# One queue's order at the end of each attention step, and who splits the last operands

## Chip, cores and metric

One core of a Trainium2 chip runs the whole program. The time is the device time of one execution in microseconds (us); the kernel before has a median of 931.12 us over three runs (930.95 to 933.09).

## What is computed

Attention with capped scores, then a feed-forward block with a gate. With q, k, v of 8 batches x 12 heads x 448 rows x 64:

```python
scores = cap * tanh((q @ k.T) / 8 / cap)
attn = softmax(scores)                     # plus 1e-9 in the denominator
x = concat_heads(attn @ v)                 # 8 x 448 x 768
x_prev = x shifted by one row in each sequence, zero first
xk = mu_k * x + (1 - mu_k) * x_prev
xr = mu_r * x + (1 - mu_r) * x_prev
k = relu(xk @ w_k)                         # 768 -> 1024
out = sigmoid(xr @ w_r) * (k * k @ w_v)    # 1024 -> 768
```

Products are made at more than single-pass accuracy: each operand is split into a high part and a remainder, and three products are summed.

## The kernel before

The first half of the program, some 560 us, is attention with the product xk @ w_k folded in. It runs in steps i = 0 to 54. A step works on several pairs of heads at once (48 pairs, six to a batch): scores, tanh, exponential and row sums of pair i, the product with v and the reciprocal sums of pair i-1, normalising and mixing of pair i-2. The key product "K" of a batch follows about seven steps behind. TensorE does scores (`s`, L211), values (`pv`, L238 and L246) and K (`kps`, L369). ScalarE does tanh (L219), exponential (L229), the old half of the mix (`pv<-x`, L290), relu (`ko`, L376) and issues the stores of k (L382). VectorE does row sums (`r<-p`, L255), the reciprocal (`sr`, L264), normalising (`x<-pv,r`, L280), the mix (`xk`, L295) and the new half of the gate operand (`xg`, L307). GpSimd splits q, k and xk (`xkh`, `xkl`) and makes the old half of `xg` (L313). The second half, from 564 us, is the two large products with w_v and w_r (`ps`, L561), with weights in seven combinations of quadrants.

Every engine takes its instructions in order, and the order within a step is written out by hand in the tables `STEP`, `STEP_0` (steps 0 to 5), `STEP_6` (6 to 13) and `STEP_2`. SyncE's queue holds nearly all transfers. Those of a step, in order:

- `gather` (L260): four transfers that bring the row sums `r` of the pair before to one place, `sq`. The reciprocal waits for them; they wait for the last row sums `red3` of the step before.
- `load_v` (L165), `weight_load` (L400, L405; steps 0 to 41).
- `rec_store` (L271), after the reciprocal; `load_qk` (L161); `rec_load` (L276, two transfers), which brings the reciprocals back spread over partitions, for normalising in the next step.
- `x_store`, at the end of the step: it stores the gate operand `xg` of pair i-2 (L324), or for the first twelve and the last two pairs x itself (L326). It waits for `gate_new`, the last VectorE instruction of the step.
- `weight_store` (L466), and in steps 43 to 46 `quad_load` (L663): two loads of quadrants of w_v per step, 384 KB each.

The next step's `gather` comes behind all of these. The program gives its transfers eight completion semaphores in turn, SyncE's and ScalarE's counted together, and a transfer is issued only when the one eight places ahead of it has landed.

Quadrants are summed on VectorE (`quad_sum`, L670, four subtractions in step 46 and four in step 48), and the sums are split by ScalarE (high, L676) and VectorE (low, L677): 14 splittings, three before step 49, four after it, four in step 50 at the places called `prep`, and the last three in a row at the end of step 50. The last four use quadrants P1 and P2, loaded by `w2_load` (L481) when step 48 opens the tail.

Of the kernel before, what the change touches and what calls it, by code (L numbers as in the profile page):

```python
# [21 lines left out]
NF = DF // 128  # L22
ND = DM // 128
NT = B * S
NPAIR = B * NP
HN = DM // 2
# [12 lines left out]
QUADS = REST[-1] + 2  # L39
# [14 lines left out]

STEP = """gather load_v weight_load weight_low S0 S1 V S2 f f f f f tanh0 exp0 red0
weight_sum tanh1 exp1 red1 norm recip rec_store K qk_high qk_low tanh2 relu mix_old k_store prep mix_new x_high x_low gate_old
K exp2 red2 weight_rest weight_sum relu k_store prep S3 K prep K tanh3 exp3 red3 gate_new relu k_store prep
weight_abs load_qk rec_load tail_open x_store weight_store quad_load"""  # L60
STEP_2 = STEP.replace("K qk_high", "K S3 qk_high").replace("prep S3 K", "prep K")
STEP_0 = """gather load_v weight_load weight_low S0 S1 V S2 f f f f f norm tanh0 exp0 red0
weight_sum tanh1 exp1 red1 recip rec_store K qk_high qk_low tanh2 relu exp2 mix_old k_store mix_new x_high x_low gate_old
K red2 weight_rest weight_sum relu k_store S3 K K tanh3 exp3 red3 gate_new relu k_store weight_abs load_qk rec_load x_store weight_store"""
STEP_6 = """gather load_v weight_load weight_low S0 S1 V S2 f f f f f norm tanh0 exp0 red0
weight_sum tanh1 exp1 K relu_early qk_rise tanh2 relu exp2 mix_old k_store mix_new red1 recip rec_store qk_low x_high x_low gate_old
K red2 weight_rest weight_sum relu k_store S3 K K tanh3 exp3 red3 gate_new relu k_store weight_abs load_qk rec_load x_store weight_store"""


def f(ap):  # L70
    return ap.bitcast(F32)


class Body:
# [437 lines left out]
    def half(self, u):  # L512
        return (NF if u < NU else ND) // 2
# [140 lines left out]
    def quad_load(self, j):  # L654
        if j == 0:
            w = lambda: self.wp.tile([P, WC, 2], U32, name="w64", bufs=3).rearrange("p n t -> p (n t)").bitcast(F32)
            half = lambda name, t, bufs: [f(self.wp.tile([P, WC], t, name=name, bufs=bufs)).rearrange("p (f n) -> p f n", f=2) for _ in range(2)]
            whole = [w().rearrange("p (f n) -> p f n", f=NF // 2) for _ in range(3)]
            self.quad = [[x[:, k:k + 2] for k in (0, 2)] for x in whole] + [half("wsq", F32, 3), half("wa", U32, 2)]
        k = j // 2  # L660
        for q in ((0, 1), (2, 3))[j % 2]:
            c, h = ND + q // 2 * (NF // 2) + 2 * k, (0, 1, 1, 0)[q]
            self.nc.sync.dma_start(self.quad[q][k], self.w_d[c:c + 2, :, h * HN:(h + 1) * HN].rearrange("c p n -> p c n"))  # L663
            self.summed = [0, 0]

    def quad_sum(self, j):
        k = j // 2
# [17 lines left out]

    def step(self, i, KS):

        nk = 0
        if self.maxima and i < NPAIR:
            self.row_maxima(i)  # L690
        pair = dict(load_qk=i + 3, qk_high=i + 2, qk_low=i + 2, qk_rise=i + 2, load_v=i, S=i, tanh=i, exp=i, red=i)
        pair.update(dict.fromkeys("V gather recip rec_store rec_load".split(), i - 1))
        pair.update(dict.fromkeys("norm mix_old mix_new x_high x_low gate_old gate_new x_store".split(), i - 2))
        for op in (STEP_0 if i < 6 else STEP_6 if i < REST[0] else STEP_2 if i % NP == 2 else STEP).split():
            j = pair.get(op)
            op, g = (op[:-1], (int(op[-1]),)) if op[-1].isdigit() else (op, ())
            if op in pair:
                j = pair[op] if j is None else j
                if 0 <= j < NPAIR:
                    getattr(self, dict(S="scores", V="values").get(op, op))(j, *g)  # L700
            elif op == "K":
                n = ((i - LAG) * 4 + nk + 1) * KS
                if 0 <= n < B * NF * ND * 3:
                    self.kpart(n, n + KS)
                nk += 1
            elif op == "tail_open":
                self.tail_open(i)
            elif op == "f":
                if i in (QUADS + 3, QUADS + 5):
                    self.quad_sum(i - QUADS - 3)  # L710
                elif i <= NPAIR:
                    self.fill()
            elif op == "quad_load":
                if QUADS <= i < QUADS + 4:
                    self.quad_load(i - QUADS)
            elif op == "relu_early":
                if i % NP == 2:
                    self.relu()
            elif op == "weight_load":
                if i in KEYS or i in REST:  # L720
                    self.weight_load()
            else:
                getattr(self, op)()

    def run(self):
# [7 lines left out]
        with ExitStack() as outer:  # L733
            def pool(name, bufs, stack=outer, **kw):
                return stack.enter_context(tc.tile_pool(name=name, bufs=bufs, **kw))
# [40 lines left out]
            tail = NPAIR + 1  # L776
            self.later, self.prep_now = [], False
            first = -12
            tiles = dict(right, reuse_waits="tile")

            def tail_open():
                ast.close()
                self.w2v = {"l": pool("w2vl", 1, **tiles)}
                self.w2_pool("v", "l", self.w2v)
                for q in (0, 3):
                    for k in (0, 2):
                        self.w2_load("v", q, slice(k, k + 2))
            self.open_tail = tail_open
            for i in range(NPAIR + LAG):
                if i == tail:  # L790
                    est.close()
                    self.w2v["h"] = pool("w2vh", 1, **tiles)
                    self.w2_pool("v", "h", self.w2v)
                    self.w2 = self.w2_splits()
                    for _ in range(3):
                        next(self.w2)
                self.prep_now = i == tail + 1
                self.step(i, KS)
                if i == tail + 1:
                    assert len(list(self.w2)) == 3  # L800
                    wst.close()
                    ust.close()
                    self.srcp = pool("srcp", 2, **tiles)
                    self.sp = pool("sp", 1, **tiles)
                    self.evp = pool("evp", 1, **tiles)
                    self.opp = pool("opp", AHEAD + 1, **tiles)
                if i == tail + 2:
                    sst.close()
                    self.ps_2 = pool("ps2", 6, space=PSUM, **right)
                if i == tail:  # L810
                    for _ in range(4):
                        next(self.w2)
                if i == NPAIR // 2 and not self.maxima:
                    self.small = nc.values_load(self.flag, min_val=0, max_val=1)
                if i > tail + 1:
                    for g in range(first, min(first + 4, 0)):
                        self.ahead(g)
                    first += 4
            assert first >= 0
            self.k_store()  # L820
            kst.close()
            w2r = pool("w2r", 1)
# [77 lines left out]
```

## Time and profile before

| | us |
|---|---|
| median of three runs | 931.12 |
| the profiled execution | 929.66 |
| its span on the core | 927.7 |
| TensorE busy in the span | 891.2 (96%) |
| VectorE, ScalarE, GpSimd busy | 738.4, 639.6, 386.0 |

The 1.96 us between span and execution lie outside what the profile shows. Busy times of TensorE are modelled, since matmuls overlap; idle times in front of an instruction are given with what ended them. In a timeline row stand the start in us, the duration in us, engine, line, operation, tile written and tiles read, shape, and in brackets the idle time of the engine before it and what released it. "SPq" and "ACTq" are transfers being issued by SyncE and ScalarE.

### The profile page before, as it was taken

To read this page: it belongs to the slowest core of one execution; us is meant where nothing else is said; L and a number is where in the kernel's file an instruction comes from. 1 tells how busy PE (TensorE), PEld (TensorE's weight loads), DVE (VectorE), ACT (ScalarE), POOL (GpSimd) and SP (SyncE) were. 2 spreads that over 40 slices of the span, in tenths; PEclk is the share of its full clock that TensorE was granted. 3 is DMA by queue.
4 is the path that set the end of the run, shared out by engine and by line. 5 is a ranking of instruction groups with operands and counts; after the bars stand their busy time and mean duration, and the time that the engine had idled before them with its cause. 6 is when DMAs were issued, how large, how long until landed. Compare 5 with 4: busy or idle time off the path is not lost.

```text
span 927.7 us, 15107 instructions
## 1 busy us (share of the span) xinstructions
PE 891.2 (96%) x4986; PEld 714.5 (77%) x4986; DVE 738.4 (80%) x1254; ACT 639.6 (69%) x946; POOL 386.0 (42%) x330
## 2 busy tenths in 40 slices
PE   6888999999999999999998899999999999999997
PEld 3336666666676666677665589999999999999996
DVE  7999986888888888888867776788887766777775
ACT  7898887887878888877866565565655535555553
POOL 5574564666676766666654220000000013344430
PEclk9899999999999999999999999999999999999999
DMA  4556655666666666656555464754455636666773
GB/s 148 169 173 188 211 161 172 194 200 204 187 195 217 209 195 217 196 177 208 191 167 181 132 215 141 261 171 147 152 162 165 196 104 206 214 212 217 222 216 117
DMA packets 123655, 171.94 MB, mean 185 GB/s; under 512 B 22576, under 2 KB 107696, under 8 KB 123568
## 3 DMA queue, kind: packets, MB, share of 16 engines
q1 hardware_dynamic: 114352, 156.21, 53.7%
q10 hardware_dynamic: 9216, 14.68, 4.2%
q8 instruction: 41, 0.67, 0.3%
q14 instruction: 46, 0.38, 0.1%
HBM read 111.48 MB, written 56.60 MB: 181 GB/s over the span
## 4 chain that ended last, share of the span: by engine, by line
PE 41%; POOL 17%; DVE 11%; DMA 9%; issue 9%; ACT 6%; SPq 6%; ACTq 0%; DVEq 0%; POOLq 0%
PE ps L561 38%; POOL xg L313 4%; DMA sq<-r 4%; SPq L260 4%; POOL qkl L98 4%; POOL xkl L98 3%; DVE r L255 3%; POOL wsq L446 2%; ACT p L219 2%; ACT p L229 2%; POOL qkh L88 2%; POOL xkh L88 2%; DMA w<-wk 2%; PE kps L369 2%; DVE sr L264 2%
## 5 line engine op out<-in xcount | busy, mean ns | idle before, releaser
L255 DVE TRANSPOSE_TENSOR_REDUCE r<-p 128x28 f32<-128x896 f32 (+1 forms) x240 | 215.3, 912 | 12.0 <-ACT p L229 9.0
L229 ACT ACTIVATE p<-p,cap_t 128x896 f32<-128x896 f32 x192 | 182.2, 949 | 10.8 <-DMA sq<-r 4.6
L219 ACT ACTIVATE p<-s,scl_t 128x896 f32<-128x896 f32 x192 | 172.9, 901 | 17.8 <-PE s L211 12.7
L369 PE MATMUL kps<-xkh,wkh 128*128 128x448 f32 x372 | 140.5, 378 | 2.3 <-ACT ko L376 2.3
L369 PE MATMUL kps<-xkl,wkh 128*128 128x448 f32 x372 | 136.0, 366 | 0.9 <-POOL xkl L98 0.9
L369 PE MATMUL kps<-xkh,wkl 128*128 128x448 f32 x372 | 136.0, 366 | 0.1
L561 PE MATMUL ps<-wvh,hi 128*128 128x384 f32 x392 | 131.0, 334 | 0.0
L561 PE MATMUL ps<-wvl,hi 128*128 128x384 f32 x392 | 130.9, 334 | 0.0
L238 PE MATMUL pv<-p,rv 128*64 128x448 f32 x576 | 125.3, 572 | 4.5 <-DVE xk L295 4.5
L545 ACT CAST hi<-s 128x512 fp32r<-128x512 f32 (+1 forms) x112 | 63.6, 568 | 90.9 <-PE ps L561 79.0
L525 POOL TENSOR_TENSOR s<-src 128x384 f32<-128x384 f32 x14 | 14.3, 1019 | 258.6 <-DVE lo L546 258.6
L546 DVE TENSOR_TENSOR lo<-s,hi 128x512 fp32r<-128x512 f32 (+1 forms) x112 | 70.1, 625 | 59.9 <-ACT hi L545 43.8
L98 POOL TENSOR_TENSOR qkl<-rqk,qkh 128x960 fp32r<-128x960 f32 x47 | 106.9, 2274 | 11.6 <-ACT qkh L92 8.3
L211 PE MATMUL s<-qkh 64*128 64x448 f32 (+1 forms) x336 | 84.6, 444 | 21.6 <-ACT p L219 15.9
L211 PEld LDWEIGHTS s<-qkh 64*128 64x128 f32 (+1 forms) x336 | 36.8, 187 | 81.0 <-ACT p L219 34.6
L446 POOL TENSOR_TENSOR wsq<-wa,wsq 128x384 f32<-128x384 f32 (+1 forms) x39 | 43.8, 1123 | 132.8 <-DVE wsq L439 132.8
L561 PE MATMUL ps<-wrh,hi 128*128 128x384 f32 x294 | 98.6, 335 | 0.3 <-DVE o L584 0.3
L561 PE MATMUL ps<-wrl,hi 128*128 128x384 f32 x294 | 98.5, 335 | 0.0
L238 PEld LDWEIGHTS pv<-p,rv 128*64 128x64 f32 x576 | 38.7, 142 | 68.6 <-issue 58.8
L545 ACT CAST hi<-src 128x512 fp32r<-128x512 f32 (+1 forms) x84 | 47.7, 568 | 62.8 <-PE ps L561 59.8
L369 PEld LDWEIGHTS kps<-xkh,wkh 128*128 128x128 f32 x372 | 69.8, 188 | 21.3 <-issue 13.1
L561 PE MATMUL ps<-wvh,lo 128*128 128x384 f32 x392 | 83.7, 334 | 0.0
(101 smaller groups left out, 1787.3 us busy)
## 6 DMA issues: line engine op xcount, KB each, us to landing
rqk<-qk SPq DMA_DIRECT2D x47, 480.0 KB
k_d<-ko ACTq DMA_DIRECT2D x64, 224.0 KB
src<-k_d SPq DMA_DIRECT2D x56, 256.0 KB
rv<-v SPq DMA_DIRECT2D x48, 256.0 KB
r<-rec_d SPq DMA_DIRECT2D x96, 112.0 KB
v_d<-o SPq DMA_DIRECT2D x56, 192.0 KB
src<-x_d SPq DMA_DIRECT2D x42, 256.0 KB
vl<-v_d SPq DMA_DIRECT2D x56, 192.0 KB
```

What stands on the lines that cost most here:

```text
L88: self.nc.gpsimd.tensor_scalar(out, x, 1.0, 0.0, op0=ALU.mult, op1=ALU.add)
L98: {"p": self.nc.gpsimd, "v": self.nc.vector}[e].tensor_sub(*a)
L211: nc.tensor.matmul(s[:, h, 0:S], qk[a][p, k], qk[b][p, 0:S], start=(n == 0), stop=(n == 2))
L219: self.nc.scalar.activation(p32, self.S.pop((i, g))[:, :n, 0:S], AF.Tanh, scale=self.scl_t)
L229: self.nc.scalar.activation(p32, p32, AF.Exp, scale=1.0 if self.maxima else self.cap_t)
L238: nc.tensor.matmul(pv[p, 0:S], v[:, g, h, :], ph[:, h, :], start=(g == 0), stop=False)
L255: self.nc.vector.tensor_reduce(out=out, in_=p32[p, h].rearrange("p h (b k) -> p (h b) k", k=32), axis=mybir.AxisListType.X, op=ALU.add, ap ...
L369: nc.tensor.matmul(self.kps[fc][:, 0:S], w, m[:, dc, :], start=first, stop=last)
L446: {"p": self.nc.gpsimd, "v": self.nc.vector}[e].tensor_add(sq, f(a), sq)
L545: self.nc.scalar.copy(hi, x)
L546: self.nc.vector.tensor_sub(lo, x, f(hi))
L561: self.nc.tensor.matmul(o, a[:, c, :], w[:, c, :], start=first and k == 0, stop=last and k == len(todo) - 1, skip_group_check=True)
```

## The change

- `quad_load` now issues one load each time it is called and stands twice in the step: behind `gather` and `load_v`, and again behind `rec_load`. The order of the eight loads is the same.
- `x_store` moves out of the end of the step, to behind `gather` and `load_v` of the next one (with i-3 for i-2).
- In step 49, the last with an `xk`, the high part is made by ScalarE and the low part by VectorE; before, both by GpSimd.
- The loads of P1 and P2 are issued after step 49's splittings in the program, not when the tail opens; `prep` also runs in step 51, so three splittings that ran in a row at the end of step 50 stand behind a relu of step 51.

```diff
-STEP = """gather load_v weight_load weight_low S0 S1 V S2 f f f f f tanh0 exp0 red0
+STEP = """gather load_v quad_load x_store weight_load weight_low S0 S1 V S2 f f f f f tanh0 exp0 red0
...
-weight_abs load_qk rec_load tail_open x_store weight_store quad_load"""
+weight_abs load_qk rec_load quad_load tail_open weight_store"""
...
-        k = j // 2
-        for q in ((0, 1), (2, 3))[j % 2]:
-            c, h = ND + q // 2 * (NF // 2) + 2 * k, (0, 1, 1, 0)[q]
-            self.nc.sync.dma_start(self.quad[q][k], self.w_d[c:c + 2, :, h * HN:(h + 1) * HN].rearrange("c p n -> p c n"))
-            self.summed = [0, 0]
+        k, q = divmod(j, 4)
+        c, h = ND + q // 2 * (NF // 2) + 2 * k, (0, 1, 1, 0)[q]
+        self.nc.sync.dma_start(self.quad[q][k], self.w_d[c:c + 2, :, h * HN:(h + 1) * HN].rearrange("c p n -> p c n"))
+        self.summed = [0, 0]
...
-        pair.update(dict.fromkeys("norm mix_old mix_new x_high x_low gate_old gate_new x_store".split(), i - 2))
+        pair.update(dict.fromkeys("norm mix_old mix_new x_high x_low gate_old gate_new".split(), i - 2))
+        pair["x_store"] = i - 3
...
+                if i == NPAIR + 1 and op in ("x_high", "x_low"):
+                    g = ("s",) if op == "x_high" else ("v",)
...
-                    self.quad_load(i - QUADS)
+                    self.quad_load(2 * (i - QUADS) + nq)
+                    nq += 1
...
-                for q in (0, 3):
-                    for k in (0, 2):
-                        self.w2_load("v", q, slice(k, k + 2))
...
-                self.prep_now = i == tail + 1
+                self.prep_now = i in (tail + 1, tail + 2)
                 self.step(i, KS)
                 if i == tail + 1:
-                    assert len(list(self.w2)) == 3
...
                 if i == tail:
                     for _ in range(4):
                         next(self.w2)
+                    for q in (0, 3):
+                        for k in (0, 2):
+                            self.w2_load("v", q, slice(k, k + 2))
```

SyncE's queue before, from the end of step 43 (store of the gate operand and two quadrant loads) through step 44:

```order
L276 DMA r<-rec_d_108 64x448 x2
L324 DMA x_d<-xg 128x448
L663 DMA w_5295<-w_d 128x2x384
L663 DMA w_5296<-w_d 128x2x384
L260 DMA sq_204<-r_1_200 32x112 x4
L165 DMA rv<-v 128x512
L271 DMA rec_d_109<-rs 28x32
L161 DMA rqk<-qk 128x960
L276 DMA r<-rec_d_109 64x448 x2
```

The same place in the changed program:

```order
L276 DMA r<-rec_d_108 64x448 x2
L662 DMA w_5197<-w_d 128x2x384
L260 DMA sq_204<-r_1_200 32x112 x4
L165 DMA rv<-v 128x512
L662 DMA w_5198<-w_d 128x2x384
L324 DMA x_d<-xg 128x448
L271 DMA rec_d_109<-rs 28x32
L161 DMA rqk<-qk 128x960
L276 DMA r<-rec_d_109 64x448 x2
```

Between `rec_load` and the four gathers one load stands where a store and two loads stood; the store and the other load are behind the gathers.

ScalarE before, from the mix of step 49 (`pv<-x_163`) to the second pair of relus of the last batch; `wvh` are high parts of quadrant sums, `ko` are relus:

```order
L290 ACTIVATE pv<-x_163,om_k 128x448
L676 CAST wvh_5836<-w_5295 128x768
L676 CAST wvh_5833<-w_5296 128x768 x2
L676 CAST wvh_5838<-wsq 128x768 x2
L676 CAST wvh_5834<-w_5297 128x768 x2
L676 CAST wvh_5832<-wvl_5816 128x768 x2
L676 CAST wvh_5835<-wvl_5819 128x768 x2
L376 ACTIVATE ko<-kps 128x448 x2
L382 DMA k_d<-ko 128x448 x2
L376 ACTIVATE ko<-s 128x448 x2
```

The same place in the changed program:

```order
L290 ACTIVATE pv<-x_163,om_k 128x448
L92 CAST xkh<-xk 128x448
L675 CAST wvh_5831<-w_5196 128x768
L675 CAST wvh_5828<-w_5197 128x768 x2
L675 CAST wvh_5833<-wsq 128x768 x2
L675 CAST wvh_5829<-w_5198 128x768 x2
L675 CAST wvh_5827<-wvl_5816 128x768
L376 ACTIVATE ko<-kps 128x448 x2
L382 DMA k_d<-ko 128x448 x2
L675 CAST wvh_5827<-wvl_5816 128x768
L675 CAST wvh_5830<-wvl_5819 128x768 x2
L376 ACTIVATE ko<-s 128x448 x2
```

Eight splittings and the new `xkh` stand ahead of the first relus, where eleven splittings stood; three follow the relus.

## Rows read from the trace of the kernel before

**Rows 1.** Stretches: duration, then busy us (instructions) of PE, PEld, DVE, ACT, POOL; clock; DMA.

```profile
60.00:140.00 80.00, 74.62 (x421) 48.86 (x423) 71.83 (x110) 70.03 (x87) 45.44 (x36) 1.00 0.58 185
140.00:460.00 320.00, 319.44 (x1800) 217.29 (x1797) 270.35 (x462) 259.72 (x334) 209.19 (x171) 1.00 0.62 199
460.00:560.00 100.00, 90.88 (x483) 67.73 (x483) 71.31 (x97) 62.81 (x85) 37.29 (x31) 1.00 0.54 173
```

**Rows 2.** Timeline of TensorE, 455 to 566 us: the rows with idle time before them.

```profile
475.81 2.48 PE L238 MATMUL pv<-p,rv 128*64 128x448 f32 x12 [0.26 <-DVE xk L295]
...
487.97 0.47 PE L211 MATMUL s<-qkh 64*128 64x448 f32 x2 [1.49 <-ACT p L219]
...
501.31 2.48 PE L238 MATMUL pv<-p,rv 128*64 128x448 f32 x12 [2.16 <-DVE xk L295]
...
514.51 0.47 PE L211 MATMUL s<-qkh 64*128 64x448 f32 x2 [2.55 <-ACT p L219]
...
524.92 2.48 PE L238 MATMUL pv<-p,rv 128*64 128x448 f32 x12 [0.67 <-DVE xk L295]
...
544.65 0.47 PE L369 MATMUL kps<-xkl,wkh 128*128 128x448 f32 x1 [0.93 <-POOL xkl L98]
...
549.22 0.47 PE L369 MATMUL kps<-xkh,wkh 128*128 128x448 f32 x1 [1.06 <-ACT ko L376]
```

**Rows 3.** Timeline of SyncE's queue, end of step 43 and gather of step 44.

```profile
476.53 1.13 SPq L276 DMA_DIRECT2D r<-rec_d  x2
480.49 0.33 SPq L324 DMA_DIRECT2D x_d<-xg  x1
480.90 0.93 SPq L663 DMA_DIRECT2D w<-w_d  x2
481.88 2.44 SPq L260 DMA_DIRECT2D sq<-r  x4
484.43 0.53 SPq L165 DMA_DIRECT2D rv<-v  x1
```

**Rows 4.** Timeline of VectorE, steps 43 to 45.

```profile
475.68 2.41 DVE L255 TRANSPOSE_TENSOR_REDUCE r<-p 128x28 f32<-128x896 f32 x3
479.06 1.39 DVE L307 SCALAR_TENSOR_TENSOR xg<-x,mu_r,xg 128x448 f32<-128x448 f32 x1 [0.98 <-POOL xg L313]
...
486.30 0.61 DVE L264 TENSOR_REDUCE sr<-sq 32x28 f32<-32x448 f32 x1 [3.31 <-DMA sq<-r]
...
494.69 0.58 DVE L280 TENSOR_TENSOR x<-pv,r 128x448 f32<-128x448 f32 x1
499.50 0.61 DVE L264 TENSOR_REDUCE sr<-sq 32x28 f32<-32x448 f32 x1 [4.23 <-DMA sq<-r]
```

**Rows 5.** Timeline of ScalarE, step 44, then the last splittings.

```profile
480.96 1.05 ACT L376 ACTIVATE ko<-kps 128x448 f32<-128x448 f32 x2
483.02 0.64 ACT L290 ACTIVATE pv<-x,om_k 128x448 f32<-128x448 f32 x1 [1.01 <-DVE x L280]
485.50 0.81 ACTq L382 DMA_DIRECT2D k_d<-ko  x2
486.36 1.04 ACT L229 ACTIVATE p<-p,cap_t 128x896 f32<-128x896 f32 x1 [2.70 <-DMA sq<-r]
...
545.70 3.03 ACT L676 CAST wvh<-wvl 128x768 fp32r<-128x768 f32 x4
548.63 0.96 ACT L376 ACTIVATE ko<-kps 128x448 f32<-128x448 f32 x2
```

**Rows 6.** Chain of work that ended last: start, us; a transfer runs to its landing.

```profile
78.42 4.95 DMA w<-wk
...
481.38 4.04 DMA w<-w_d
...
509.21 2.78 DMA rv<-v
```

**Rows 7.** Waits in the whole span: total us, times, longest.

```profile
ACT wsq L412 <- DMA w<-wk: 8.9, 7, 2.2
```

More of the change, by code (lines that the diff above doesn't have):

```diff
@@ L50 @@
 LATE = [*range(12), NPAIR - 2, NPAIR - 1]
-STEP = """gather load_v weight_load weight_low S0 S1 V S2 f f f f f tanh0 exp0 red0
+STEP = """gather load_v quad_load x_store weight_load weight_low S0 S1 V S2 f f f f f tanh0 exp0 red0
 weight_sum tanh1 exp1 red1 norm recip rec_store K qk_high qk_low tanh2 relu mix_old k_store prep mix_new x_high x_low gate_old
 K exp2 red2 weight_rest weight_sum relu k_store prep S3 K prep K tanh3 exp3 red3 gate_new relu k_store prep
-weight_abs load_qk rec_load tail_open x_store weight_store quad_load"""
+weight_abs load_qk rec_load quad_load tail_open weight_store"""
 STEP_2 = STEP.replace("K qk_high", "K S3 qk_high").replace("prep S3 K", "prep K")
-STEP_0 = """gather load_v weight_load weight_low S0 S1 V S2 f f f f f norm tanh0 exp0 red0
+STEP_0 = """gather load_v x_store weight_load weight_low S0 S1 V S2 f f f f f norm tanh0 exp0 red0
 weight_sum tanh1 exp1 red1 recip rec_store K qk_high qk_low tanh2 relu exp2 mix_old k_store mix_new x_high x_low gate_old
-K red2 weight_rest weight_sum relu k_store S3 K K tanh3 exp3 red3 gate_new relu k_store weight_abs load_qk rec_load x_store weight_store"""
-STEP_6 = """gather load_v weight_load weight_low S0 S1 V S2 f f f f f norm tanh0 exp0 red0
+K red2 weight_rest weight_sum relu k_store S3 K K tanh3 exp3 red3 gate_new relu k_store weight_abs load_qk rec_load weight_store"""
+STEP_6 = """gather load_v x_store weight_load weight_low S0 S1 V S2 f f f f f norm tanh0 exp0 red0
 weight_sum tanh1 exp1 K relu_early qk_rise tanh2 relu exp2 mix_old k_store mix_new red1 recip rec_store qk_low x_high x_low gate_old
-K red2 weight_rest weight_sum relu k_store S3 K K tanh3 exp3 red3 gate_new relu k_store weight_abs load_qk rec_load x_store weight_store"""
+K red2 weight_rest weight_sum relu k_store S3 K K tanh3 exp3 red3 gate_new relu k_store weight_abs load_qk rec_load weight_store"""
 def f(ap):
@@ L686, in step @@
     def step(self, i, KS):
-        nk = 0
+        nk = nq = 0
         if self.maxima and i < NPAIR:
@@ L818, in run @@
                     first += 4
-            assert first >= 0
+            assert first >= 0 and next(self.w2, None) is None
             self.k_store()
```

## The prediction, made before the changed kernel ran

> **What bounds the kernel now.** I read the busy times by stretch first. From 140 to 460 us TensorE is busy 319.44 of 320 us: nothing done to the queues there can be worth more than 0.56 us. From 60 to 140 us it lacks 5.38 us, and from 460 to 560 us, where the last pairs pass and the quadrants of w_v are loaded, 9.12 us [rows 1]. After that comes the second half, which the change does not touch. So the 9.12 us are nearly the whole prize. TensorE's timeline splits them into seven waits: values in steps 44, 46 and 48 wait for `xk` (0.26, 2.16, 0.67), scores of steps 45 and 47 wait for a tanh (1.49, 2.55), and in the last batch one K matmul waits for `xkl` (0.93) and one for a relu (1.06) [rows 2]. These seven add up to 9.12.
>
> Next, what ends late behind these waits. The reciprocal of step 44 stands 3.31 us at its gathered sums, and that of step 45 4.23 us [rows 4]; `xk` is made right behind it. The row sums that the gather of step 44 reads end at 475.68 + 2.41 = 478.09 [rows 4], but the gather is issued only at 481.88, because SyncE first waits for `gate_new` (it ends at 480.45 [rows 4]), then issues the store and two quadrant loads (0.33 and 0.93 us) and only then the four gathers (2.44 us) [rows 3]. So the gather is 3.8 us late for a store and for loads that nobody needs until step 46. A second path runs over ScalarE: its two stores of k in step 44 could go when the mix ends, 483.02 + 0.64 = 483.66, and go at 485.50 [rows 5]. By the program's turn of eight semaphores the first of them waits for the second quadrant load, which lands at 481.38 + 4.04 = 485.42 [rows 6]. The exponential behind them starts 2.70 us late [rows 5], and the tanh for which scores wait 1.49 us comes right after it.
>
> **The change part by part.** *Store and loads behind the gathers, steps 43 to 46.* The gather of step 44 can now go once `rec_load` (476.53 + 1.13 = 477.66 [rows 3]) and one load of some 0.45 us are issued: at about 478.2 for 481.88, and step 43's own gather gains as much in the same way, so I count 3.7 us or more per step. The reciprocal waits of 3.31 and 4.23 us then end earlier than their cover, which is the row sums and the normalising ahead of them on VectorE. Eight places ahead of step 44's stores of k now stand its gathers, issued by 480.7, so ScalarE's stall goes too: the exponential starts at 480.96 + 1.05 + 0.64 + 0.81 = 483.46, less 0.26 because TensorE is that much earlier, 483.2 for 486.36 [rows 2, 5].
>
> What is late next? Step 45's normalising ended 494.69 + 0.58 - 486.36 = 8.9 us behind that exponential [rows 4, 5]; now at 483.2 + 8.9 = 492.1. The reciprocal, its two small followers and the mix follow without a wait; in the trace they took from 499.50 to the values at 501.31, which `xk` released, so 1.81 us [rows 2, 4], and `xk` now ends at 493.9. TensorE took 501.31 - 475.81 = 25.5 us from the values of step 44 to those of step 46, and without its waits of 1.49 and 2.16 us 21.85. It starts 0.26 us sooner, at 475.55, so it comes there at 497.4 [rows 2]. The 2.16 us go, with 3.5 us to spare. The 2.55 us in step 47 are different: step 46 has four quadrant sums on VectorE ahead of the normalising, which stay. In the trace the scores at 514.51 start 13.2 us after `xk` of step 45 (values at 501.31 were released by it), and TensorE alone would need 10.65 (13.2 less its wait of 2.55) [rows 2]. They stop waiting once `xk` is 2.55 us ahead of the values, and I have 3.5. That is a margin of 0.9 us, so I leave 0.3 of the 2.55 and keep the whole 2.55 as the other end. Step 48's 0.67 hangs on the `xk` made behind step 47's exponential, and goes with that.
>
> *High part on ScalarE, low part on VectorE in step 49.* `xkl` costs 0.93 us today [rows 2]. TensorE now comes there 7.13 us sooner (0.26 + 1.49 + 2.16 + 2.55 + 0.67), and the `xk` that is split sooner by about as much (7.4 us in step 45: 493.9 for 501.31), so on GpSimd the lateness would stay about as it is. The edit puts a cast on ScalarE and a subtraction on VectorE instead; by the mix of the same 128x448 on ScalarE, 0.64 [rows 5], and the normalising on VectorE, 0.58 [rows 4], they take 1.2 us in a row. Both stand ahead of splittings, so neither queues. I count the 0.93 as gained; the other end is 0.
>
> *Three splittings behind a relu.* A splitting on ScalarE takes 3.03 / 4 = 0.76 us [rows 5]; three are 2.3 us. Eleven of them ran ahead of the relu at 548.63, for which TensorE waited 1.06 [rows 2]. TensorE and ScalarE both come there sooner by about the same, and ScalarE has the cast of 0.64 more: without the move 1.06 + 0.64 = 1.7 us of wait would stay, with it 1.7 - 2.3, so none. Moving the loads of P1 and P2 in the program changes their place in SyncE's queue only by one store of 0.33 us [rows 3], against a landing of 4.04 for such a load [rows 6]. I leave 0.2 for this part; the other end is the 1.06.
>
> *Store behind the gathers, steps 0 to 13.* Here ScalarE waits seven times for weights of w_k, 8.9 us in all [rows 7]. What stands ahead of that load in the queue is the same set of transfers, so its issue time stays, but the store's 224 KB now stand directly ahead of it. From a 256 KB load that lands 2.78 us after its issue and a 768 KB load that lands after 4.95 [rows 6], 224 KB are worth at most (4.95 - 2.78) x 224 / 512 = 0.95 us per load. At the least it is nothing, since the voice load ahead goes out earlier by the store's issue. I take 0.1, near the least: 7 x 0.1 = 0.7 us lost; the bound is 6.7. The Trainium skill, "DMA: Bandwidth & Descriptors", section "Issuing engines are not separate DMA queues", says that all transfers run on the same 16 engines and interleave, whoever starts them. By that rule moving a transfer only moves whose bytes go first, and the sum would take the 6.7 in full.
>
> *Steady steps 14 to 42.* TensorE has no idle time to give back. The store now needs its data behind gathers and v load, 2.44 + 0.53 us after the row sums [rows 3]; `gate_new` ends 480.45 - 478.09 = 2.4 us behind them [rows 4]. So it does not hold up what follows. I count nothing.
>
> **Sum.** 9.12 - 0.3 - 0.2 - 0.7 = 7.9 us. The profiled execution would fall from 929.66 (its span from 927.7) to 921.8. It lies 1.46 under the median of the runs, 931.12, so the median would be 923.2 us.
>
> **Rivals.** (1) *VectorE's loop in step 46.* If `xk` of step 45 is not 2.55 us ahead (a gather that lands late behind a quadrant load, as now), the wait of 2.55 stays, and being later ScalarE also keeps a relu wait of 1.06: 7.9 - 2.25 - 0.86 = 4.8 gained, 926.3 us. For it: the margin is 0.9 us. Against it: only one load, not two, stands ahead of a gather, and that is issued 3.7 us sooner. (2) *Weights in the first steps come late.* The store's bytes cost their full 6.7 in place of 0.7: 929.2 us, no change. Against it: the v load ahead is earlier by the same place in the queue. By the rule of the Trainium skill above this is the outcome; no row of the trace shows which of two transfers went first. (3) *The landing was late, not the queue.* If a gather lands when it does now whatever its issue, because a quadrant load's data is ahead of it either way, only the last two waits of rows 2 (0.93, 1.06) go: 929.8 with the 0.7 lost, no change. Against it: four issues take 2.44 us by themselves. (4) *Slower.* The store stands ahead of weight load and `rec_store` and waits for `gate_new`, which hangs on GpSimd. If that were later than the 3.0 us of gathers and v load, every microsecond would hold up 28 steady steps without slack: at 1 us, 28 lost, 951 us; it decides from (7.9 / 28 =) 0.3 us. Against it: `gate_new` ends 2.4 us behind the row sums in rows 4, with 0.98 us of waiting for GpSimd in it.
>
> **How the numbers follow.** Forecast 0.70 (921.5 to 925), rival 1 0.16, rival 2 0.05, rival 3 0.04, rival 4 0.05. About 0.3% (2.8 us, so 928.3 and 933.9) is what a measurement here can tell from no change. Faster 0.88 (forecast, rival 1, and rival 2 in part), same 0.07, slower 0.05. The range reaches down to all of 9.12 gained plus a little from the first steps, 920.8, and up past rival 1 with a start cost of 2 us, 927.8; that leaves out rivals 2 to 4.
>
> **What would show it.** TensorE idle from 460 to 560 us should be under 1 us of 100; the reciprocal's waits for gathered sums gone or under 1 us; ScalarE's stores of k in step 44 issued within 0.2 us of the mix; no relu wait after 549. Rival 1 shows as a tanh wait of over 2 us in front of step 47's scores; rival 2 as weight waits of 12 us or more on ScalarE in place of 8.9 and more idle time of TensorE from 60 to 140 us; rival 3 as gathers that still land behind a quadrant load; rival 4 as idle time of TensorE between 140 and 460 us. I would be wrong most likely in the 0.9 us margin and in the 0.1 per weight load.

## The result, and the profile of the changed kernel

The changed kernel takes 922.84 us (median of 4 runs, 921.98 to 924.59) where the kernel before takes 932.11 (4 runs, 930.95 to 933.42): ratio 0.9899, 95% interval 0.9873 to 0.9924. Two further sets of runs of it gave 924.34 (ratio 0.9908) and 924.21 (0.9901). The forecast was 923.2. The gain beside the kernel before is 9.27 us, where 7.9 was forecast.

The stretches of [rows 1], in the profile of the changed kernel (duration, busy us and instructions of PE, PEld, DVE, ACT, POOL, clock, DMA):

```profile
60.00:140.00 80.00, 72.06 (x394) 46.37 (x395) 68.42 (x103) 66.23 (x81) 43.28 (x34) 0.98 0.56 177
140.00:460.00 320.00, 319.95 (x1814) 219.00 (x1813) 275.16 (x468) 263.71 (x338) 212.02 (x175) 1.00 0.64 201
460.00:560.00 100.00, 100.00 (x537) 77.64 (x536) 73.83 (x105) 70.16 (x98) 33.44 (x28) 1.00 0.58 181
```

From 460 to 560 us TensorE is now busy without a gap: all seven waits of [rows 2] are gone. From 60 to 140 us it lacks 7.94 us where it lacked 5.38, at a granted clock of 0.98 there and 1.00 before. SyncE's queue, from the end of step 43 to the store in step 44 (answers [rows 3]):

```profile
474.67 1.12 SPq L276 DMA_DIRECT2D r<-rec_d  x2
475.88 0.54 SPq L662 DMA_DIRECT2D w<-w_d  x1
476.51 2.44 SPq L260 DMA_DIRECT2D sq<-r  x4
479.05 0.53 SPq L165 DMA_DIRECT2D rv<-v  x1
479.68 0.38 SPq L662 DMA_DIRECT2D w<-w_d  x1
480.15 0.42 SPq L324 DMA_DIRECT2D x_d<-xg  x1
```

The gathers go 0.72 us behind the end of `rec_load`, in place of 4.22 us (481.88 - 477.66), and the store finds its data ready. VectorE's reciprocals follow the normalising without a wait, answering [rows 4]:

```profile
481.58 0.59 DVE L280 TENSOR_TENSOR x<-pv,r 128x448 f32<-128x448 f32 x1
482.09 0.59 DVE L264 TENSOR_REDUCE sr<-sq 32x28 f32<-32x448 f32 x1
...
492.93 0.59 DVE L280 TENSOR_TENSOR x<-pv,r 128x448 f32<-128x448 f32 x1
493.44 0.59 DVE L264 TENSOR_REDUCE sr<-sq 32x28 f32<-32x448 f32 x1
```

On ScalarE the stores of k in step 44 go at once, and the exponential behind them follows the mix without the 2.70 us of [rows 5]:

```profile
482.66 0.33 ACTq L382 DMA_DIRECT2D k_d<-ko  x1
483.03 0.63 ACT L290 ACTIVATE pv<-x,om_k 128x448 f32<-128x448 f32 x1
483.17 0.33 ACTq L382 DMA_DIRECT2D k_d<-ko  x1
483.59 1.03 ACT L229 ACTIVATE p<-p,cap_t 128x896 f32<-128x896 f32 x1
```

### The profile page after: what moved, and what is told of

It reads as the page before. It is cut to its first block, busy times and chain, and to the rows that moved or that the text cites. A ratio compares the mean times of both kernels' runs of the same rounds, so it can differ in the third digit from the quotient of the medians.

```text
span 920.2 us, 15151 instructions
## 1 busy us (share of the span) xinstructions
PE 887.3 (96%) x4986; PEld 714.8 (78%) x4986; DVE 738.4 (80%) x1255; ACT 641.6 (70%) x947; POOL 383.4 (42%) x328
## 4 chain that ended last, share of the span: by engine, by line
PE 85%; DVE 6%; DMA 3%; ACT 3%; issue 1%; SPq 1%; DVEq 0%; ACTq 0%
PE ps L561 39%; PE kps L369 23%; PE s L211 11%; PE pv L238 10%; DVE r L255 3%; PE pv L246 2%; DMA w<-wk 2%; ACT p L219 1%; ACT p L229 1%; PE s L369 1%; DMA w<-wr 1%; DVE sr L264 0%; DVE wkl L460 0%; DVE wa L435 0%; DMA r<-rec_d 0%
## 5 line engine op out<-in xcount | busy, mean ns | idle before, releaser
L369 PE MATMUL kps<-xkh,wkh 128*128 128x448 f32 x372 | 140.3, 377 | 1.0 <-ACT ko L376 1.0
L369 PE MATMUL kps<-xkh,wkl 128*128 128x448 f32 x372 | 136.1, 366 | 0.1
L369 PE MATMUL kps<-xkl,wkh 128*128 128x448 f32 x372 | 136.0, 366 | 0.0
L238 PE MATMUL pv<-p,rv 128*64 128x448 f32 x576 | 122.9, 563 | 2.4 <-DVE xk L295 2.4
L238 PEld LDWEIGHTS pv<-p,rv 128*64 128x64 f32 x576 | 38.0, 140 | 64.5 <-issue 57.0
L369 PEld LDWEIGHTS kps<-xkh,wkh 128*128 128x128 f32 x372 | 69.8, 188 | 19.9 <-issue 12.5
```

What stands on the lines that cost most here:

```text
L238: nc.tensor.matmul(pv[p, 0:S], v[:, g, h, :], ph[:, h, :], start=(g == 0), stop=False)
L369: nc.tensor.matmul(self.kps[fc][:, 0:S], w, m[:, dc, :], start=first, stop=last)
```

## Where the time went, stretch by stretch

TensorE's timeline gives four marks in every trace: where the values (L238) of steps 14, 42 and 48 start, and where the last K matmul (L369) starts. All kernels of this study are below, each from its profiled execution. "Store" says where `x_store` stands in steps 0 to 13; the column "14 to 42" and those behind it are differences of the marks in us.

| kernel | store, steps 0 to 13 | values of 14 at | 14 to 42 | 42 to 48 | 48 to last K | last K to span's end |
|---|---|---|---|---|---|---|
| before | end of step | 150.17 | 303.80 | 70.95 | 38.79 | 363.99 |
| tail_only | end of step | 154.04 | 305.25 | 70.84 | 39.50 | 365.57 |
| quad_only | end of step | 152.78 | 305.60 | 66.85 | 37.72 | 365.05 |
| start_old | end of step | 152.24 | 302.52 | 63.06 | 36.61 | 365.37 |
| changed | ahead of w_k | 153.41 | 302.04 | 63.05 | 36.62 | 365.08 |
| after_again | ahead of w_k | 152.53 | 301.91 | 63.06 | 36.61 | 365.79 |
| after_third | ahead of w_k | 157.60 | 301.92 | 63.05 | 36.82 | 364.21 |
| store_only | ahead of w_k | 153.68 | 301.92 | 63.05 | 37.72 | 365.33 |
| no_quad | ahead of w_k | 154.49 | 301.92 | 63.16 | 38.57 | 365.16 |
| no_prep | ahead of w_k | 154.35 | 302.15 | 63.05 | 38.38 | 365.07 |
| no_xsplit | ahead of w_k | 155.81 | 301.92 | 63.05 | 36.61 | 365.51 |
| start_behind | behind w_k | 152.39 | 301.92 | 63.05 | 36.61 | 364.53 |
| start_first | behind w_k and v | 152.83 | 301.92 | 63.05 | 36.54 | 365.86 |
| first_again | behind w_k and v | 151.12 | 302.44 | 63.05 | 36.54 | 364.15 |

Three things are to be seen. With the store moved in the steady steps, the column 14 to 42 differs by no more than 0.6 us among eleven executions, and 42 to 48 by 0.1, so small differences there mean something. In the first column they don't: after_again and after_third, the same instructions, differ by 5 us. And the last column, where all kernels run the same program, has a spread of 1.9 us by itself. A part of the spread in the first column is TensorE's granted clock, one row each for after_again and after_third (stretch, duration, busy us and instructions by engine, clock, DMA):

```profile
0.00:150.00 150.00, 128.64 (x668) 76.07 (x669) 126.55 (x208) 125.24 (x153) 81.93 (x74) 0.95 0.56 170
```

```profile
0.00:150.00 150.00, 123.12 (x643) 71.26 (x645) 125.49 (x205) 120.48 (x148) 79.78 (x73) 0.93 0.54 166
```

The same row gives a mean clock of 0.97 for before, changed and start_old, 0.94 for no_prep and 0.95 for all others. By these two rows the difference is 0.02 x 150 = 3 us of full clock, an estimate, so up to 3 of the 5 us between these two may be the clock; the rest is open, and so is why the clock differs.

Of the 7.5 us between the spans of before and changed (927.7 and 920.2), +3.24 come from the first 14 steps, -1.76 from steps 14 to 42, -7.90 from 42 to 48, -2.17 from the last batch and +1.09 from the rest.

## Experiments

**The parts one by one: store_only.** The store alone is moved, in all steps.

```diff
-STEP = """gather load_v weight_load weight_low ...
+STEP = """gather load_v x_store weight_load weight_low ...
-... rec_load tail_open x_store weight_store quad_load"""
+... rec_load tail_open weight_store quad_load"""
...
+        pair["x_store"] = i - 3
```

> Kernel before with the store alone moved (all steps); quadrant loads, split and splittings as before. Theory (the order of the queue): the gather of step 44 goes behind rec_load and two quadrant loads, about 478.7 instead of 481.88 us, and the reciprocal's waits of 3.31 and 4.23 us shrink below 1 us; the first five of the seven waits (7.13 us) go, xkl 0.93 and relu 1.06 stay, and the first steps cost 1.65 us as in the changed kernel: 5.5 gained of 931.1, 925.6 us (ratio 0.994). Rival (quadrant data ahead of the gather is what delays it, not the wait for gate_new): gathers land as now, only the cost of the first steps is left, 932.8 us (1.002).

Measured: 923.55 us (5 runs, 923.42 to 926.26), ratio 0.9906 (0.9883 to 0.993). Steps 42 to 48 take 63.05 us, exactly what they take in the changed kernel, so there the store alone is the whole gain, quadrant loads or not; the rival falls. It is also 2 us better than the theory said (3 us by the ratio, 0.9906 for 0.994), and the table shows most of the reason: steps 14 to 42 take 301.92 us instead of 303.80, a gain that nobody had on the bill. One wait is left, a relu's:

```profile
541.60 0.47 PE L369 MATMUL kps<-xkh,wkh 128*128 128x448 f32 x1 [0.85 <-ACT ko L376]
```

**quad_only.** The loads alone are split and moved.

```diff
-STEP = """gather load_v weight_load ...
+STEP = """gather load_v quad_load weight_load ...
-... rec_load tail_open x_store weight_store quad_load"""
+... rec_load quad_load tail_open x_store weight_store"""
...
```

> Kernel before with the quadrant loads alone split and moved; the store stays at the end of the step. Theory: the gather still stands behind a store that waits for gate_new at 480.45, so it goes at about 480.8 instead of 481.88, 1.1 us sooner in each of four steps: 2 to 4 us gained and no cost in the first steps, 927 to 929 us (0.996 to 0.998); ScalarE's stores of k in step 44 no longer wait for a quadrant load. Rival (the loads, not the store, are the whole cause): all 7.1 us of the first five waits go, 924.0 us (0.992).

Measured: 929.34 us (10 runs), ratio 0.9957 (0.9941 to 0.9972), close to the theory's 0.996 to 0.998: steps 42 to 48 take 66.85 us, 4.1 less, and steps 14 to 42 gain nothing (305.60).

**tail_only.** The split of the last `xk` and the three splittings, together with the later loads of P1 and P2, with the other transfers as before.

```diff
+                if i == NPAIR + 1 and op in ("x_high", "x_low"):
+                    g = ("s",) if op == "x_high" else ("v",)
...
-                self.prep_now = i == tail + 1
+                self.prep_now = i in (tail + 1, tail + 2)
...
```

> Kernel before with the split of the last xk on ScalarE and VectorE and the three splittings behind a relu, queues as before. Theory: the two waits in the last batch (0.93 for xkl, 1.06 for relu) go and the other five stay: 2.0 gained, 929.1 us (0.998). Rival (these two edits only matter once the queue is repaired, or move the wait to the next relu): 931.1 us (1.000).

Measured: 933.6 us (12 runs), ratio 0.9997 (0.998 to 1.0014): the rival is right. The last batch takes 39.50 us where it took 38.79. The wait for `xkl` is gone, but the two relu waits that stand there now are 2.47 us together, and the two old waits were 1.99:

```profile
554.16 0.47 PE L369 MATMUL kps<-xkh,wkh 128*128 128x448 f32 x1 [1.76 <-ACT ko L376]
...
562.43 0.47 PE L369 MATMUL kps<-xkh,wkh 128*128 128x448 f32 x1 [0.71 <-ACT ko L376]
```

The second of them is new. In the chain of waits its relu follows on ScalarE a store of k that is issued only when an earlier one has landed, 6.82 us after its issue, as the turn of eight semaphores would have it.

**no_quad: the changed kernel with the loads as before**, two in a row at the end of the step.

```diff
-STEP = """gather load_v quad_load x_store ...
+STEP = """gather load_v x_store ...
-... rec_load quad_load tail_open weight_store"""
+... rec_load tail_open weight_store quad_load"""
...
```

> Changed kernel with the quadrant loads as before, two in a row at the end of the step. Theory (the store's wait was the whole cause): values of step 48 come 63.05 us after those of step 42, as in the changed kernel, and TensorE has no idle time from 460 to 560 us; 923 us, ratio 0.990, as the changed kernel beside it. Rival (the split loads carry part of the gain, with the store moved too): the gathers stand behind 0.9 us of loads and the reciprocal waits 0.5 us and more; 1 to 2 us slower than the changed kernel.

Measured: 924.99 us (6 runs, ratio 0.9921) beside 924.21 of the changed kernel; the times alone don't tell the two apart. Up to step 48 the theory holds (63.16). Then the rival does: the last batch is 1.96 us longer (38.57 against 36.61), with relu waits of 0.74 and 0.98 us, and the reciprocal of step 47 waits 1.11 us:

```profile
542.41 0.47 PE L369 MATMUL kps<-xkh,wkh 128*128 128x448 f32 x1 [0.74 <-ACT ko L376]
...
550.95 0.47 PE L369 MATMUL kps<-xkh,wkh 128*128 128x448 f32 x1 [0.98 <-ACT ko L376]
```

```profile
517.25 0.61 DVE L264 TENSOR_REDUCE sr<-sq 32x28 f32<-32x448 f32 x1 [1.11 <-DMA sq<-r]
```

The chain of waits of that trace shows the way there, from the last gather of step 47 on:

```profile
512.80 0.59 SPq L260
...
513.43 3.70 DMA sq<-r
...
517.25 0.62 DVE sr L264
...
523.81 1.79 DMA sq<-r
...
532.49 6.36 DMA wvl<-w_d
...
542.81 7.09 DMA k_d<-ko
```

The gather lands 3.70 us after its issue, behind the data of two quadrants; one step later, with no quadrant ahead, the same transfer takes 1.79 us. Through the reciprocals and the normalising of step 48 the last splittings and the first relus are late. From there the chain goes on over a load of P1 or P2 (6.36 us), the splittings and relus, and a store of k that lands after 7.09 us; the next store of k waits for it, and the relu of the second wait stands behind that store. So the third rival of the prediction, landing and not queue, was right for the gathers here: those of steps 44 to 46 also land late (3.22, 4.02 and 4.72 us), but only the 1.11 us reach TensorE. The loads' share of the change is the last batch, some 2 us, not steps 43 to 47.

**no_prep: the changed kernel without the move of the three splittings**; the loads of P1 and P2 are issued when the tail opens again, too.

```diff
-                self.prep_now = i in (tail + 1, tail + 2)
+                self.prep_now = i == tail + 1
...
                 if i == tail + 1:
+                    assert len(list(self.w2)) == 3
...
```

> Changed kernel without the move of the three splittings. Theory by the prediction: ScalarE has 2.3 us of splittings more ahead of the first relu of the last batch, and TensorE waits there 1.7 us (1.06 as before and 0.6 for the cast of the high part); with the store moved alone it was 0.85, so 0.85 + 0.6 = 1.4 us by that trace. 924.3 us. Rival (TensorE and ScalarE are both so much sooner that nothing is late): no wait, 923 us.

Measured: one run, 924.8 us. The theory holds: the first relu wait is 1.30 us for its 1.4. The relu waits come to 1.52 us, and the last batch takes 38.38 us, 1.77 more than with the move:

```profile
542.95 0.47 PE L369 MATMUL kps<-xkh,wkh 128*128 128x448 f32 x1 [1.30 <-ACT ko L376]
550.73 0.47 PE L369 MATMUL kps<-xkh,wkh 128*128 128x448 f32 x1 [0.22 <-ACT ko L376]
```

**no_xsplit: the changed kernel with both halves of the last `xk` on GpSimd.**

```diff
-                if i == NPAIR + 1 and op in ("x_high", "x_low"):
-                    g = ("s",) if op == "x_high" else ("v",)
```

> Changed kernel with GpSimd making both halves of the last xk. Theory by the prediction (the split is as late as before against a TensorE that is earlier by as much): one K matmul waits 0.93 us for xkl. Rival (with the store moved alone no K matmul waited for xkl): no wait, and the relu comes 0.57 us sooner.

Measured: one run, 924.66 us, with 36.61 us in the last batch, as with the split, and no wait of TensorE:

```profile
460.00:560.00 100.00, 100.00 (x540) 76.52 (x539) 74.89 (x104) 69.57 (x95) 38.16 (x31) 1.00 0.59 183
```

The split is worth nothing once the store is moved; the rival is right. The first relu comes even 1.37 us sooner after the values of step 48, not 0.57 (19.23 us after them, 20.60 in the changed kernel), since ScalarE need not wait for `xk` and cast it.

**The first steps: start_old.** The changed kernel, with the store back at the end of the step in steps 0 to 13.

```diff
-STEP_0 = """gather load_v x_store weight_load ...
+STEP_0 = """gather load_v weight_load ...
-... load_qk rec_load weight_store"""
+... load_qk rec_load x_store weight_store"""
...
-        pair["x_store"] = i - 3
+        pair["x_store"] = i - 2 if i < REST[0] else i - 3 if i > REST[0] else -1
```

> Changed kernel with the store back at the end of the step in steps 0 to 13 only. Theory (the store's bytes directly ahead of w_k's load delay the weights by 0.6 to 0.7 us per load): ScalarE's waits for weights fall from 12.4 back to about 9 us, values of step 14 come at about 150 us instead of 153.4, and the 1.65 us that the first 24 steps cost come back: ratio to before 0.988 where the changed kernel has 0.990, some 921.2 us. Rival (the earlier gathers in the first steps are worth as much as the weights lose): 922.8 us (0.990).

Measured: 921.78 us (6 runs, 920.93 to 925.48), ratio 0.9882 (0.9859 to 0.9905). The time is near the theory's, but the trace does not bear it out: values of step 14 come at 152.24, not 150, and ScalarE waits 12.2 us for weights, not 9. That the first column of the table differs so much among executions was not seen until here, and the 1.65 us of these expectations had been read from a single pair of traces. The next three runs ask it again.

**after_again and after_third** are the changed kernel, unchanged.

> The changed kernel once more, as the measure for the two beside it and for how much the first steps differ from one execution to the next. In four executions with the first steps of the kernel before, values of step 14 came at 150.2, 152.2, 152.8 and 154.0 us; in two with the store moved at 153.4 and 153.7. If the move costs a fixed 1.65 us there, they come at 153.4 again (153.2 to 153.8); if the spread between executions is as large as the cost, anywhere from 151 to 155. Ratio 0.988 to 0.992 either way, some 923 us.

> The changed kernel, as the measure beside the next three on the same chip. From values of step 14 to values of step 42 it took 302.0 and 301.9 us in two traces, where three kernels that keep the store at the end of the step took 303.8, 305.6 and 305.3: 301.9 to 302.2 again if that is the queue's order and not chance. About 923 us, ratio 0.990.

Measured: 924.34 us (6 runs, 921.51 to 926.06) and 924.21 us (6 runs, 921.07 to 925.41). Values of step 14 came at 152.53 and at 157.60: the spread is larger than the cost looked for. Steps 14 to 42 took 301.91 and 301.92.

**start_behind.** The store stands behind the load of w_k.

```diff
-STEP_0 = """gather load_v x_store weight_load ...
+STEP_0 = """gather load_v weight_load x_store ...
...
```

> Changed kernel with the store behind the load of w_k, not ahead of it, in steps 0 to 13. Theory (a transfer lands behind the bytes issued ahead of it): the load of w_k takes 4.95 to 5.1 us again, not 5.6 to 5.9, ScalarE's waits for weights are some 5 us less in all, and values of step 14 come at 151.5 to 152.5 us; 921.5 us, ratio 0.988. Rival (all transfers share the engines, so the load is as late with the store behind it): landing after 5.6 to 5.9 us as in the changed kernel, 923 us.

Measured: 921.27 us (6 runs, 919.91 to 923.57), ratio 0.9879 (0.9846 to 0.9911), 3 us less than the changed kernel beside it, though the intervals of the two ratios overlap. The load of w_k in the chain of waits (start, us to landing), first in the changed kernel, then in start_old, then in start_behind:

```profile
67.53 5.65 DMA w<-wk
...
115.76 5.64 DMA w<-wk
```

```profile
68.51 4.98 DMA w<-wk
...
115.26 5.00 DMA w<-wk
```

```profile
68.75 5.14 DMA w<-wk
...
115.11 5.26 DMA w<-wk
```

In these three traces such a load lands 0.6 to 0.7 us later with the store ahead of it, and 0.1 to 0.4 later with the store behind it. That is the theory, with a small part of the rival in it. In the chains of waits of all traces the 768 KB loads take 4.88 to 5.25 us with the store at the end of the step, and 5.47 to 6.21 with the store ahead, except for the one issued at 91 to 93 us, which takes 6.63 to 7.82 in three traces.

**start_first and first_again.** The load of w_k also ahead of the load of v; the same kernel twice.

```diff
-STEP_0 = """gather load_v x_store weight_load ...
+STEP_0 = """gather weight_load load_v x_store ...
...
```

> Changed kernel with the load of w_k also ahead of the load of v in steps 0 to 13 (gathers, w_k, v, store). Theory: the 256 KB of v no longer stand ahead of the weights, so they land about 0.7 to 1 us sooner again, counted from the gathers, ScalarE's weight waits fall below 6 us in all and values of step 14 come at 149 to 151 us; 920 us, ratio 0.986. Rival (ScalarE's weights aren't what sets the pace of the first steps; TensorE waits there for tanh and xk, which hang on something else): waits for weights fall and values of step 14 stay at 152 to 154 us; 922.5 us.

> The kernel with the load of w_k right behind the gathers in steps 0 to 13, once more: it had a median of 920.5 us beside 924.3 of the changed kernel. If that is real, 2 to 4 us less than the changed kernel beside it, ratio 0.986 to 0.988. If it was the spread of the first steps (values of step 14 came at 152.8 against 152.5), the two agree within 1 us.

Measured: 920.5 us (6 runs, 918.84 to 922.88), ratio 0.9866 (0.9833 to 0.99), and 919.15 us (5 runs, 918.98 to 921.03), ratio 0.9859 (0.9837 to 0.9882). That is 3.8 and 5.1 us less than the changed kernel beside it, and the fastest version of this study; all runs of first_again lie below all runs of the changed kernel beside it. ScalarE's waits for weights, in start_first and then in first_again, against 8.9 us in [rows 7] and 12.4 in the changed kernel:

```profile
ACT wsq L412 <- DMA w<-wk: 5.6, 5, 1.5
```

```profile
ACT wsq L412 <- DMA w<-wk: 4.1, 4, 2.1
```

Values of step 14 come at 152.83 and 151.12. The waits for weights fall as the theory says, the mark comes later than it says: in these two traces the weights are no longer what holds the first steps most. In their chains of waits from 36 to 150 us no load of w_k is left, and the load of v, now behind it, has come in, three times and two; the longest in start_first:

```profile
79.78 5.23 DMA rv<-v
```

What sets the spread of the first steps, beside the clock, stays open.

## Why the prediction was right, and where it was not

**The late gathers: right, with one name too many.** The seven waits went; the 0.9 us margin in step 47 held, and the 0.3 and 0.2 us that were left in place went too. The prediction gave the gain to "store and loads behind the gathers" together. store_only shows that the store alone does it up to step 48, and no_quad that the loads act in the last batch. The stretch gained 7.90 us where the waits shown in it are 7.13 (0.26 + 1.49 + 2.16 + 2.55 + 0.67): step by step, the distance between values shrank by up to 0.3 us more than the wait in the row. Idle time in front of an instruction understated here what the wait cost; matmul ends are modelled, which may be why.

**Steady steps: the step that failed most.** "TensorE has no idle time to give back", it says, and: "I count nothing." The three traces with the old store need 303.8 to 305.6 us for steps 14 to 42, all eleven with the moved one 301.9 to 302.5. So 1.8 us are gained on the profiled execution and 2.8 between the means (304.9 and 302.1). The busy share of [rows 1] (319.44 of 320) was read as a bound of 0.56 us on any gain there; 1.76 us came. The chain of waits of the kernel before says otherwise, and the prediction did not read it there. The page's part on the chain, by engine, before and then after:

```profile
PE 41%; POOL 17%; DVE 11%; DMA 9%; issue 9%; ACT 6%; SPq 6%; ACTq 0%; DVEq 0%; POOLq 0%
```

```profile
PE 85%; DVE 6%; DMA 3%; ACT 3%; issue 1%; SPq 1%; DVEq 0%; ACTq 0%
```

In the kernel before, the chain runs through a ring that has no matmul in it. Two steps of it, early in the "full" stretch:

```profile
183.95 1.39 POOL xg L313
...
194.50 1.40 POOL xg L313
...
195.92 0.69 DVE xg L307
...
196.88 0.08 SPq L324
...
197.49 0.54 SPq L260
...
199.35 2.49 DMA sq<-r
...
201.96 0.62 DVE sr L264
...
203.15 0.57 DVE xk L295
...
203.80 0.57 POOL xkh L88
...
205.61 1.39 POOL xg L313
```

From 194.50 on this is one turn of the ring: gate operand, store, gather, reciprocal, `xk`, its split, next gate operand, 11.11 us. The 10.55 us before it the chain spends on GpSimd alone. Such pairs of steps start at 161.98, 183.95 and 205.61, and the last ends at 227.95: 65.97 us for six steps. The values of steps 17 to 23 are 65.95 us apart in that trace (183.37 and 249.32) and 64.55 in the changed kernel (186.43 and 250.98). So the ring sets the pace there, and what it is longer than TensorE's own work is lost; TensorE catches up none of it. 1.58 of the 1.76 us are lost by step 23; from there to step 42 the two kernels differ by 0.18, with the store still in its old place. tail_only and quad_only show the same (100.24 and 100.46 us for steps 14 to 23, 97.44 in after_again). What differs is the landing of the gathers in the chain: 2.49 to 3.21 us up to 221 us, 1.76 to 2.13 from 270 to 460; what delays the early ones stays open. The store was the ring's link from VectorE to SyncE, and moving it behind the gathers opens the ring. The fourth rival, that the store would hold up the steady steps, was the wrong way round: it did so before.

**First steps: right place, wrong size.** 0.1 us per load was taken "near the least", of a bound of 0.95. Measured are 0.6 to 0.7 us (5.57 to 5.65 for 4.94 to 5.02), and up to 1.2 in other traces with the store ahead. The reason given, that the load of v goes out earlier, does not help: what counts is the bytes issued ahead. With the store behind the load most of the loss is gone. By the rule of the Trainium skill that the prediction weighed ("DMA: Bandwidth & Descriptors", section "Issuing engines are not separate DMA queues"), the store's bytes would be paid in full, 6.7 us. The landing times lie nearer to that than to 0.1 us per load, and the 0.1 to 0.4 us with the store behind fit its word that transfers interleave. In the end time less is seen. The seven traces with the store ahead of w_k reach step 14 at 154.55 on average, the seven others at 152.22: 2.3 us, with single traces overlapping. The mean granted clock up to 150 us is 0.949 in the first seven and 0.956 in the others, so up to 1 of the 2.3 us may be the clock.

**Last batch: right sum, wrong parts.** 0.93 + 0.86 = 1.79 us were forecast, 2.17 came. But the split of `xk`, put at 0.93, is worth nothing: the prediction let the last `xk` come sooner by no more than TensorE, 7.1 us, and it comes 8.7 us sooner (532.03 for 540.73) where TensorE comes 6.4 sooner (values of step 48). Taking out the move of the splittings (put at 0.86) costs 1.77, and taking out the place of the loads (not on the bill) 1.96, each from a single trace beside 36.61 to 36.82 in three of the changed kernel. These two don't add up: with the store alone moved the batch takes 37.72, only 1.1 more than with everything. The tail edits without the moved loads make it longer, by 0.71 us with the store in its old place (tail_only) and by 0.85 with the store moved (no_quad against store_only). They pay only together with the loads.

**Why the number fits.** 923.2 was forecast and 922.84 came, but that is in part luck: errors of both signs met. The first steps lose 2.3 us on average (3.24 in the profiled pair) where 0.7 was put, and the steady steps give 1.8 to 2.8 where nothing was. Steps 42 to 48 gave 7.90 for 6.83 and the last batch 2.17 for 1.79, and 1.09 were lost in the second half, where nothing was changed. The medians of before moved too, from 931.12 to 932.11. The profiled execution of before, from which the sum was made, also had the earliest step 14 of all 14 traces (150.17).

## What to carry to other kernels

Look for a ring in the chain of waits before a busy share of 99% is taken for "nothing to gain": if the ring that releases the busy engine is as long as that engine's own pace, every delay in it is paid. Compare such a stretch step by step between two traces: it shows where the loss lies. In a queue that is worked off in order, put what others wait for first and what only has to be done sometime, above all a store that itself waits, behind it; then price the bytes ahead of each load that is waited for, also of those that the move newly puts there. And before a term of one or two microseconds is read from a pair of traces, see how much that stretch differs between executions of the same kernel.

## What the runs showed of the hardware

Issue is not free: four gathers of 14 KB take SyncE 2.44 us to issue, 0.54 to 0.60 us each, and the last of them lands 1.79 us after its issue when nothing large is ahead. The Trainium skill, "DMA: Bandwidth & Descriptors", section "Issuing engines are not separate DMA queues", calls the issue time "usually small relative to the DMA itself"; for these transfers the trace differs, with a third of the landing time each.

GpSimd's split of the last `xk` beside VectorE's splittings took 1.30 and 1.74 us, and 0.57 and 1.16 us for the same shapes one step earlier (in store_only, the later pair second):

```profile
527.29 0.57 POOL L88 TENSOR_SCALAR xkh<-xk 128x448 fp32r<-128x448 f32 x1 [6.60 <-DVE xk L295]
527.94 1.16 POOL L98 TENSOR_TENSOR xkl<-xk,xkh 128x448 fp32r<-128x448 f32 x1
533.88 1.30 POOL L88 TENSOR_SCALAR xkh<-xk 128x448 fp32r<-128x448 f32 x1 [4.78 <-DVE xk L295]
535.26 1.74 POOL L98 TENSOR_TENSOR xkl<-xk,xkh 128x448 fp32r<-128x448 f32 x1
```

The Trainium skill, "SBUF — State Buffer", section "SBUF: two separate sides", tells of a port that the two engines share and that one holds for a whole instruction; the 0.73 us more agree with one wait behind a VectorE operation of 0.95 us. VectorE paid as well: its three splittings beside these two took 4.02 us, and 2.70 in the changed kernel, where GpSimd stood still.
